# Reordering the lead of an attention and two-MoE kernel, and rounding the first expert's weights on GpSimd

## The chip, the cores and the metric

The kernel runs on one core of a Trainium2 chip. The metric is the device time of one execution in microseconds (us), lower is better. The engines are TensorE (PE in the profile; its weight loads are PEld), VectorE (DVE), ScalarE (ACT) and GpSimd (POOL), each with its own queue of instructions that runs in order; nearly all DMAs are issued by SyncE (SP), also in order.

## The reference

Three blocks follow one another: attention over pooled keys and values, a mixture layer with a rational function, and a gated layer.

```python
# q, k, v: 8 batches, 8 heads, 576 positions, 64 wide
k_p = k.reshape(B, H, Sp, 8, D).mean(axis=3)
v_p = v.reshape(B, H, Sp, 8, D).mean(axis=3)
scores = scale * np.matmul(q, k_p.transpose(0, 1, 3, 2))
scores = scores - np.max(scores, axis=-1, keepdims=True)
attn = np.exp(scores)
attn = attn / (np.sum(attn, axis=-1, keepdims=True) + 1e-09)
x = np.matmul(attn, v_p)                       # -> 4608 tokens x 512
h = x @ w_in                                   # 512 -> 2048
g = (a0 + a1*h + a2*h*h + a3*h**3) / (1 + |b0|*|h| + |b1|*h*h + 1e-6)
x = g @ w_out                                  # 2048 -> 512
out = (sigmoid(x @ w_gate) * (x @ w_val)) @ w_out2   # 512 -> 1536 -> 512
```

The weights arrive as 64-bit numbers.

## The kernel before

**Arithmetic.** Every large product is made of three passes: a number is split into a high part that TensorE's format holds and a low part, and the products low x high, high x high and high x low are added in one PSUM bank (`mm3`, L498 to L502).

**Weights.** Each 512-column piece of a weight is loaded raw (`wi_load`, `wo_load`, 512 KB, L122 and L124 for SyncE). `conv1` turns the 64-bit words into 32-bit floats: two ScalarE operations at once (L92, L94), and, deferred to the next call of `gap()`, a shift on VectorE (L100) and an integer addition on GpSimd (L102). `conv2` makes the two parts: the high part `wh` is a ScalarE copy that rounds (L117), the low part `wl` a subtraction (L118). For the pieces of `w_in` (`wi`) the subtraction runs on VectorE, for those of `w_out` (`wo`) on GpSimd. `weights_a(p)` issues, for step p, `wi_conv2(p+3)`, `wo_conv2(p)`, `wi_conv1(p+5)`, `wo_conv1(p+2)`, `wi_load(p+8)`, `wo_load(p+5)`, in this order, as far as such pieces (0 to 15) exist.

**Steps.** Time is a list of steps written out by hand. The lead, steps -8 to -1, does the attention of the first block of 512 tokens (tiles 0 to 3 of 128 tokens, tile 4 belongs to the next block) and starts the weights. Then 144 steps follow: step n computes a hidden product of 128 x 512 (`g1`, 12 matmuls) and the second product of step n-3 (`g2`, 12 matmuls). The rational function of step n is `rational1` (ScalarE L541, L542; VectorE L543 to L545), `rational2` (ScalarE L551, L552, L554: a reciprocal by logarithm and exponential) and `rational3` (VectorE L558 to L560); `split_g` makes the parts of g (ScalarE L525, GpSimd L528) during the next step. `gap()` is called between `rational2` and `rational3`. `weights_a(n)` stands at the end of the steps 0 to 15.

**Banks.** Four PSUM banks rotate among hidden products (a bank is free when L560 is done), scores (two banks a tile, free when VectorE's L382 is done), transposes of the attention weights (two, free when ScalarE's L410 has copied them) and attention outputs.

**Attention of a tile**, over several steps: scores (L369), maximum and subtraction on VectorE (L380, L382), exponential (ScalarE L388), then `normalise`: sums, sum and reciprocal on VectorE (L395, L397, L398) and the multiply on GpSimd (L399); transposes (L406) copied by ScalarE (L410); the product with v (L421), written as two parts by ScalarE (L426) and VectorE (L427). Each piece of work has a step, a rank and a part: in the lead, part 0 of the elementwise work of a step (`run(off_pe, st, 0)`) comes before part 1. In steps 3, 6, 9 and 12 a tile is normalised, in steps 2, 5, 8 and 11 scores are taken.

**Pooling.** The keys' pooling is a VectorE reduction (L318); `pool_v0(c)` pools chunk c of the first batch's v, chunks 0 and 1 on GpSimd (L348, L349) and chunks 2 and 3 on VectorE (L351); later batches' v is pooled on GpSimd (L335, L336), two chunks of the second batch in step -1 and three in step 0, then, for the third batch, chunks from step 10 on.

**Loads at the start.** SyncE issues 13 loads of the first batch, then `RA` = 3 loads of the second batch's k, then the parameters (L761, L762); in step -7 it issues NCH = 5 further loads into buffers that the first loads leave free.

Of the kernel before, what the change touches and what calls it, by code (L numbers as in the profile page):

```python
# [13 lines left out]
AF = mybir.ActivationFunctionType  # L14
# [21 lines left out]
def attention_moe_glu_kernel(ctx: ExitStack, tc: tile.TileContext, q, k, v, w_in, w_out, ca, cb, w_gate, w_val, w_out2, out):  # L36
    nc = tc.nc
# [8 lines left out]
    NJ = H // 2  # L46
# [63 lines left out]
    def gap():  # L110
        for f in between:
            f()
        between.clear()

    def conv2(raw, wh, wl, eng=nc.gpsimd):
        t = raw[:, :, 1].bitcast(F32)
        nc.scalar.activation(wh, t, AF.Copy)  # L117
        eng.tensor_tensor(out=wl, in0=t, in1=wh.bitcast(F32), op=ALU.subtract)  # L118

    def load_raw(raw, src, by_cols):  # L120
# [48 lines left out]
    def wo_stream(f):  # L169
        wo[f] = slot(wo_tag(f), F32R, "wo")  # L170
        nc.sync.dma_start(wo[f].bitcast(F32).rearrange("p h x -> p (h x)"), wod[f])
# [59 lines left out]
    with tc.manual_schedule():  # L231
# [25 lines left out]
        RA = 3  # L257
# [6 lines left out]
        def early(shape, name):  # L264
            spare[0] = (spare[0] + 1) % len(later)
            pool, tag = later[spare[0]]
            return pool.tile(shape, F32, tag=tag, name=name)

        def load_unit(start=False, tag=None):
            if loaded[0] == len(units):  # L270
                return
            u = units[loaded[0]]
            loaded[0] += 1
            if tag:
                t = tag[0].tile([P, 4 * P], F32, tag=tag[1], name="raw1")
            elif start:
                t = early([P, 8 * P if u[0] == "v" else 4 * P], "raw0")
            else:
                t = raw_p.tile([P, 4 * P], F32, tag="raw", name="raw")
            if u[0] == "q":  # L280
                b, t0, n = tiles[u[1]]
                o = (b * S + t0) * H * D
                nc.sync.dma_start(t[:, :NJ * n], q[o:o + n * H * D].rearrange("(p x) -> p x", p=P))
            elif u[0] == "k":
                cols = k_cols(u[2])
                nc.sync.dma_start(t[:, :(cols.stop - cols.start) * POOL], k[u[1], :, cols.start * POOL:cols.stop * POOL])
            elif u[1] == 0:

                nc.sync.dma_start(t[:SP].rearrange("p (h x) -> p h x", h=2),
                                  v[0][2 * u[2]:2 * u[2] + 2].rearrange("h (s j) d -> s h (j d)", j=POOL))  # L290
            else:
                rows = v[u[1]].rearrange("h (s j) d -> (h s) (j d)", j=POOL)
                c = u[2]
                m = P if c < NCH - 1 else CL
                nc.sync.dma_start(t[:m], rows[c * P:c * P + m])
            raws[u] = t
            if not start and not tag:
                in_ring.add(u)
# [10 lines left out]
        def k_cols(c):  # L309

            return slice(c * D, min((c + 1) * D, NJ * SP))
# [137 lines left out]
        def put(step, rank, pe, rest, gen, *a, use=()):  # L449
            plan.append((step, rank, len(plan), pe, rest, gen(*a), use))  # L450
# [16 lines left out]
        s0 = at[0]  # L467
        for c in range(NCH):
            put(s0 - 4, 0, 0, 0, ew, pool_k, 0, c, use=[("k", 0, c)])
        for c in range(NJ):  # L470
            put(s0 - 2, 5, 0, c >= NJ // 2, ew, pool_v0, c, use=[("v", 0, c)])
        put(s0 - 4, 1, 0, 0, ew, place_k, 0)
        for b in range(1, B):
            e0, e1 = max(at[first[b - 1]], -2), at[last[b - 1]]
            for c in range(2 * NCH):
                w, f = (("k", pool_k), ("v", pool_v))[c // NCH]
                st = e0 + c * (e1 - (3 if w == "k" else 1) - e0) // (2 * NCH)
                if b == 1 and w == "k":
                    st = c // 2 - 4
# [7 lines left out]
        lead = plan[0][0]  # L487
# [5 lines left out]
        def run(which, step, part):  # L493
            for gen in which.get((step, part), []):
                next(gen, None)
# [37 lines left out]
        def g1(n):  # L533
            i, f = divmod(n, NF1)
            ys[n] = hidden(wi[f], xs[i])

        def rational1(n):
            h = ys[n]
            s, u, y = new_tmp("s", "su", 3), new_tmp("u", "su", 3), new_tmp("y", "y", 3)

            nc.scalar.activation(u, h, AF.Abs, scale=coef[:, 5:6])  # L541
            nc.scalar.activation(y, h, AF.Identity, scale=coef[:, 3:4], bias=coef[:, 2:3])  # L542
            nc.vector.scalar_tensor_tensor(out=u, in0=u, scalar=coef[:, 4:5], in1=h, op0=ALU.add, op1=ALU.mult)  # L543
            nc.vector.tensor_tensor(out=y, in0=h, in1=y, op=ALU.mult)
            nc.vector.scalar_tensor_tensor(out=y, in0=y, scalar=coef[:, 1:2], in1=h, op0=ALU.add, op1=ALU.mult)  # L545
            ys[n] = (h, s, u, y)

        def rational2(n):

            h, s, u, y = ys[n]  # L550
            nc.scalar.activation(u, u, AF.Abs)  # L551
            nc.scalar.activation(s, u, AF.Ln, scale=2.0 ** LSH, bias=ONE * 2.0 ** LSH)  # L552

            nc.scalar.activation(h, s, AF.Exp, scale=-1.0, bias=LSH * math.log(2.0))  # L554

        def rational3(n):
            r, s, u, y = ys[n]
            nc.vector.scalar_tensor_tensor(out=y, in0=y, scalar=coef[:, 0:1], in1=r, op0=ALU.add, op1=ALU.mult)  # L558
            nc.vector.scalar_tensor_tensor(out=r, in0=u, scalar=ONE, in1=r, op0=ALU.add, op1=ALU.mult)
            nc.vector.scalar_tensor_tensor(out=y, in0=r, scalar=-2.0, in1=y, op0=ALU.add, op1=ALU.mult)  # L560

        def split_g(n):
            y = ys.pop(n)[3]
            gs[n] = g = g_p.tile([P, 2, TB], F32R, tag="g", name="g")
            split_hi(g, y)
            split_lo(g, y, nc.gpsimd)

        def g2(n):
            i, f = divmod(n, NF1)
            if f == 0:  # L570
                new_acc(i)
            g, wt = gs.pop(n), wo[f]
            for e in range(NJ):
                es = slice(e * P, (e + 1) * P)
                mm3(acc[i][e], wt[:, 1, es], wt[:, 0, es], g[:, 1], g[:, 0], f == 0, f == NF1 - 1)

        def g2_out(n):
            i, f = divmod(n, NF1)
            if f == NF1 - 1:
                for e in range(NJ):  # L580
                    store(acc[i][e], x2d[i][:, e], e < 3, *(("su", 3) if e == NJ - 1 else ()))
# [16 lines left out]
        def ring_load(t):  # L598

            s_, j = divmod(t % (7 * NS), 7)  # L600
            if t < NP * NS * 7:
                ring[t] = wp.tile([P, 2, 4 * P], F32R, tag=f"wi{t % NQ}", name="wq")
                nc.sync.dma_start(ring[t].bitcast(F32), w2d[s_][:, 2 * j:2 * j + 2])
# [152 lines left out]
        nstart = NCH + NJ + n0  # L756
        for i in range(nstart):
            load_unit(True)
        for i in range(RA):
            load_unit()  # L760
        nc.sync.dma_start(pc[:, 0:4], ca.rearrange("(o n) -> o n", o=1).to_broadcast([P, 4]))  # L761
        nc.sync.dma_start(pc[:, 4:6], cb.rearrange("(o n) -> o n", o=1).to_broadcast([P, 2]))  # L762

        def weights_a(p):

            for ahead, f, n in ((3, wi_conv2, NF1), (0, wo_conv2, NF1), (5, wi_conv1, NF1), (2, wo_conv1, NF1),
                                (8, wi_load, NF1), (5, wo_load, NF1)):
                if 0 <= p + ahead < n:
                    f(p + ahead)

        for st in range(lead, 0):
            run(on_pe, st, 0)
            run(on_pe, st, 1)
            run(off_pe, st, 0)
            run(off_pe, st, 1)
            if st == lead + 1:

                for x in range(NCH):
                    load_unit(tag=later[4 + x])
            weights_a(st)  # L780
            gap()

        nc.scalar.activation(coef[:, 0:4], pc[:, 0:4], AF.Copy, scale=-1.0)
        nc.scalar.activation(coef[:, 4:6], pc[:, 4:6], AF.Abs)
# [1 line left out]
        for n in range(N1):  # L786
            m = n - LAG
            if n == N1 - NF1:
                att.close()
                late = ctx.enter_context(tc.tile_pool(name="late", bufs=1))  # L790
            g1(n)
            run(on_pe, n, 0)
            rational1(n)
            run(off_pe, n, 0)
            if n >= 1:
                split_g(n - 1)
            rational2(n)
            run(off_pe, n, 2)
            gap()
            rational3(n)  # L800
            if m >= 0:
                g2(m)
                g2_out(m)
            run(on_pe, n, 1)
            run(off_pe, n, 1)
            if n < NF1:
                weights_a(n)
            elif n % NF1 >= FS:
                wo_stream(n % NF1)
            background(n - NF1)  # L810
            x = n - (N1 - NF1)
            if x == 0:
                rawx = [xs_p.tile([P, 8 * TB], F32, tag="xs", name="rawx")]
                x_load(0)
            if 1 <= x <= NQ:
                ring_load(x - 1)
            if 3 <= x <= 6:
                x_prep(x - 3)
            if x in (4, 5):
                wo2_load(NF1 - NQ + x - 4)  # L820
            if x >= 7:
                wo2_load(x - 7)
# [68 lines left out]
```

## Time and profile before

| | |
|---|---|
| time, median of 3 runs | 1813.69 us (1812.81 to 1815.04) |
| profiled execution: time / span | 1815.3 us / 1813.5 us |
| mean granted TensorE clock | 0.986 |
| TensorE matmul busy | 1761.6 us (97%) |
| VectorE / ScalarE / GpSimd busy | 1104.0 / 975.8 / 801.3 us |
| the chip's DMA mean rate | 173 GB/s |

How to read it: busy times are sums over one profiled execution, and the span runs from its first to its last instruction; the device time is a little longer. The idle time of an engine costs nothing unless it is the one that holds up the others, so the stretches have to be looked at one by one. In the timelines a row has the start in us, the length (of all instructions merged in the row), the engine, the line of the kernel, the operation, what it writes and reads, how many instructions it merges, and in brackets how long the engine had been idle before it and what ended that.

### The profile page before, as it was taken

Reading aid. Unit: us, or ns where it says so; the run is one execution under the profiler, and the core shown is the slowest. Engines: PE = TensorE matmul, PEld = TensorE weight load, DVE = VectorE, ACT = ScalarE, POOL = GpSimd, SP = SyncE. Lnnn points to the kernel's source line nnn. Section 1 sums busy time; section 2 is a strip of 40 time slices with the busy share of each in tenths; the row PEclk is TensorE's granted clock in tenths of the full one; section 3 lists DMA queues with packets and bytes.
Section 4 is the critical chain, followed back from the end, with each engine's and each line's share of the span. In section 5 each row is a group of like instructions: output and inputs, shape, how many; then the busy total and the mean of one; then the engine's idle time right before and its main releaser. Section 6 shows DMA issues by size and latency. Waiting matters only on the chain. (4 is left out here: it accounts for less than half of the span.)

```text
span 1813.5 us, 25319 instructions
## 1 busy us (share of the span) xinstructions
PE 1761.6 (97%) x9056; PEld 1525.1 (84%) x9056; DVE 1104.0 (61%) x1788; ACT 975.8 (54%) x1763; POOL 801.3 (44%) x787
## 2 busy tenths in 40 slices
PE   6699999999999999999999999999999999999999
PEld 5578787788878887788878998998998998998997
DVE  6898887878888888888776333333433333433341
ACT  5998877687877777877875222222222222222221
POOL 3766554563555536634442324324324334334231
PEclk8899999999999999999999999999999999999999
DMA  8564444543544454425465753763763763763660
GB/s 258 169 202 144 151 156 145 195 152 131 202 170 156 139 193 161 168 100 176 167 221 197 236 181 128 236 182 125 240 186 120 240 197 109 238 201 106 206 198 36
DMA packets 128209, 313.60 MB, mean 173 GB/s; under 512 B 16596, under 2 KB 48340, under 8 KB 128084
## 3 DMA queue, kind: packets, MB, share of 16 engines
q1 hardware_dynamic: 128084, 311.99, 52.8%
q8 instruction: 72, 1.18, 0.3%
q14 instruction: 53, 0.43, 0.1%
HBM read 257.95 MB, written 52.95 MB: 171 GB/s over the span
## 5 line engine op out<-in xcount | busy, mean ns | idle before, releaser
L674 DVE TENSOR_TENSOR t<-h,t 128x384 f32<-128x384 f32 x360 | 200.8, 558 | 388.0 <-ACT t L682 273.0
L528 POOL TENSOR_TENSOR g<-y,g 128x512 fp32r<-128x512 f32 x144 | 187.2, 1300 | 283.8 <-ACT g L525 216.6
L727 POOL TENSOR_TENSOR t<-t 128x384 f32<-128x384 f32 x72 | 84.4, 1172 | 449.0 <-issue 253.4
L500 PE MATMUL acc<-g,wo 128*128 128x512 f32 x576 | 233.7, 406 | 0.0
L500 PE MATMUL h<-xs,wi 128*128 128x512 f32 x576 | 231.3, 402 | 2.2 <-DVE xs L427 2.0
L502 PE MATMUL acc<-g,wo 128*128 128x512 f32 x576 | 226.8, 394 | 1.3 <-POOL g L528 1.3
L501 PE MATMUL h<-xs,wi 128*128 128x512 f32 x576 | 226.5, 393 | 0.0
L502 PE MATMUL h<-xs,wi 128*128 128x512 f32 x576 | 226.4, 393 | 0.0
L501 PE MATMUL acc<-g,wo 128*128 128x512 f32 x576 | 226.0, 392 | 0.0
L502 PE MATMUL h<-xS,wq 128*128 128x384 f32 x576 | 193.4, 336 | 0.0
L500 PE MATMUL h<-xS,wq 128*128 128x384 f32 x576 | 193.2, 335 | 0.0
L501 PE MATMUL h<-xS,wq 128*128 128x384 f32 x576 | 193.0, 335 | 0.0
L541 ACT ACTIVATE u<-h,coef 128x512 f32<-128x512 f32 x144 | 98.2, 682 | 104.7 <-PE h L502 104.4
L558 DVE SCALAR_TENSOR_TENSOR y<-y,coef,h 128x512 f32<-128x512 f32 x144 | 107.4, 746 | 75.2 <-ACT h L554 73.0
L543 DVE SCALAR_TENSOR_TENSOR u<-u,coef,h 128x512 f32<-128x512 f32 x144 | 106.4, 739 | 70.9 <-ACT y L542 70.3
L500 PE MATMUL h<-xA,wq 128*128 128x384 f32 x432 | 149.4, 346 | 0.1
L502 PE MATMUL h<-xA,wq 128*128 128x384 f32 x432 | 144.9, 335 | 0.0
L501 PE MATMUL h<-xA,wq 128*128 128x384 f32 x432 | 144.9, 335 | 0.0
L500 PEld LDWEIGHTS h<-xs,wi 128*128 128x128 f32 x576 | 109.7, 191 | 26.8 <-DVE xs L427 3.0
L500 PEld LDWEIGHTS acc<-g,wo 128*128 128x128 f32 x576 | 109.0, 189 | 26.5 <-issue 4.6
L502 PEld LDWEIGHTS acc<-g,wo 128*128 128x128 f32 x576 | 108.9, 189 | 25.6 <-POOL g L528 1.7
L502 PEld LDWEIGHTS h<-xs,wi 128*128 128x128 f32 x576 | 109.3, 190 | 23.8 <-DVE xs L427 0.2
(115 smaller groups left out, 4041.2 us busy)
## 6 DMA issues: line engine op xcount, KB each, us to landing
wq<-w2d SPq DMA_DIRECT2D x252, 512.0 KB
wo<-wod SPq DMA_DIRECT2D x88, 512.0 KB
w2d<-wq SPq DMA_DIRECT2D x36, 512.0 KB
x2d<-o SPq DMA_DIRECT2D x36, 256.0 KB
out_dram<-o SPq DMA_DIRECT2D x36, 256.0 KB
raw<-in_k_dram SPq DMA_DIRECT2D x32, 256.0 KB
raw<-in_q_dram SPq DMA_DIRECT2D x32, 256.0 KB
wiraw<-in_moe_w_in_dram SPq DMA_DIRECT2D x16, 512.0 KB
```

The costliest lines, as they stand in the source:

```text
L500: nc.tensor.matmul(out_, wl, xh, start=start, stop=False, skip_group_check=on)
L501: nc.tensor.matmul(out_, wh, xh, start=False, stop=False, skip_group_check=on)
L502: nc.tensor.matmul(out_, wh, xl, start=False, stop=stop, skip_group_check=on)
L528: eng.tensor_tensor(out=g[:, 1], in0=y, in1=g[:, 0].bitcast(F32), op=ALU.subtract)
L541: nc.scalar.activation(u, h, AF.Abs, scale=coef[:, 5:6])
L543: nc.vector.scalar_tensor_tensor(out=u, in0=u, scalar=coef[:, 4:5], in1=h, op0=ALU.add, op1=ALU.mult)
L558: nc.vector.scalar_tensor_tensor(out=y, in0=y, scalar=coef[:, 0:1], in1=r, op0=ALU.add, op1=ALU.mult)
L674: nc.vector.tensor_tensor(out=out_, in0=a, in1=b, op=ALU.add)
L727: eng.tensor_tensor(out=y, in0=x, in1=y, op=ALU.mult)
```

## The change

- The high part of a `wi` piece is made by GpSimd (`tensor_copy`) where ScalarE made it (L117); VectorE subtracts as before. `wo` pieces are converted as before.
- Chunk 1 of the first batch's v is pooled in part 1 of its step, behind tile 0's normalisation, where it was in part 0, ahead of it. Both are on GpSimd.
- The three `RA` loads leave the place before the parameters and go to the end of step -7; the five NCH loads go from step -7 to the end of step -6. In both steps they now follow `weights_a`.
- `weights_a(-1)`, with `wi_conv2(2)`, `wi_conv1(4)`, `wo_conv1(1)` and the loads of wi 7 and wo 4, leaves the lead and is issued in step 0 after `rational3(0)`. The `gap()` that followed it goes too, so its shifts and additions come with those of `weights_a(0)` in the `gap()` of step 1.

```diff
     def conv2(raw, wh, wl, eng=nc.gpsimd):
         t = raw[:, :, 1].bitcast(F32)
-        nc.scalar.activation(wh, t, AF.Copy)
+        if eng is nc.gpsimd:
+            nc.scalar.activation(wh, t, AF.Copy)
+        else:
+            nc.gpsimd.tensor_copy(wh, t)
         eng.tensor_tensor(out=wl, in0=t, in1=wh.bitcast(F32), op=ALU.subtract)
...
         for c in range(NJ):
-            put(s0 - 2, 5, 0, c >= NJ // 2, ew, pool_v0, c, use=[("v", 0, c)])
+            put(s0 - 2, 5, 0, c >= 1, ew, pool_v0, c, use=[("v", 0, c)])
...
         for i in range(nstart):
             load_unit(True)
-        for i in range(RA):
-            load_unit()
         nc.sync.dma_start(pc[:, 0:4], ca.rearrange("(o n) -> o n", o=1).to_broadcast([P, 4]))
...
             run(off_pe, st, 0)
             run(off_pe, st, 1)
+            if st < -1:
+                weights_a(st)
+                gap()
             if st == lead + 1:
+                for i in range(RA):
+                    load_unit()
+            if st == lead + 2:
                 for x in range(NCH):
                     load_unit(tag=later[4 + x])
-            weights_a(st)
-            gap()
...
             gap()
             rational3(n)
+            if n == 0:
+                weights_a(-1)
             if m >= 0:
                 g2(m)
                 g2_out(m)
```

## Rows read from the trace of the kernel before

**Rows 1.** Busy time by stretch: stretch, length, busy us and count by engine, clock, DMA

```profile
38.50:63.06 24.56, 12.55 (x53) 9.39 (x53) 18.85 (x29) 20.80 (x39) 18.91 (x25) 0.71 0.52 171
63.06:180.00 116.94, 109.81 (x559) 88.56 (x559) 106.05 (x181) 107.35 (x188) 78.31 (x74) 0.95 0.53 175
180.00:300.00 120.00, 116.63 (x583) 94.65 (x582) 97.49 (x160) 92.13 (x165) 62.17 (x69) 0.99 0.47 160
```

**Rows 2.** Waits of TensorE, 63 to 160 us: us in total, times, longest

```profile
PE sc L369 <- ACT aT L410: 4.5, 3, 2.0
```

**Rows 3.** Timeline of ScalarE, steps 3, 4 and 15

```profile
72.60 0.66 ACT L117 ACTIVATE wi<-wiraw 128x512 fp32r<-128x512 f32 x1
...
75.99 0.67 ACT L541 ACTIVATE u<-h,coef 128x512 f32<-128x512 f32 x1
...
156.84 0.69 ACT L541 ACTIVATE u<-h,coef 128x512 f32<-128x512 f32 x1 [1.40 <-PE h L502]
```

**Rows 4.** Timeline of VectorE, steps 2, 3, 4 and 13

```profile
61.94 0.73 DVE L543 SCALAR_TENSOR_TENSOR u<-u,coef,h 128x512 f32<-128x512 f32 x1
...
63.97 0.42 DVE L100 TENSOR_SCALAR wiraw<-wiraw 128x512 int32<-128x512 int32 x1
...
69.52 0.75 DVE L543 SCALAR_TENSOR_TENSOR u<-u,coef,h 128x512 f32<-128x512 f32 x1 [0.61 <-ACT y L542]
...
74.74 0.73 DVE L395 TENSOR_REDUCE r<-e 64x8 f32<-64x576 f32 x1
...
77.35 0.75 DVE L543 SCALAR_TENSOR_TENSOR u<-u,coef,h 128x512 f32<-128x512 f32 x1 [0.89 <-ACT y L542]
...
145.75 0.74 DVE L543 SCALAR_TENSOR_TENSOR u<-u,coef,h 128x512 f32<-128x512 f32 x1
```

**Rows 5.** Timelines of VectorE, GpSimd and TensorE, tiles 0 and 1

```profile
15.04 0.20 DVE L398 RECIPROCAL r<-r 128x8 f32<-128x8 f32 x1
...
17.91 1.15 POOL L399 TENSOR_TENSOR e<-e,r 128x576 f32<-128x576 f32 x1
21.53 1.15 POOL L399 TENSOR_TENSOR e<-e,r 128x576 f32<-128x576 f32 x1 [2.47 <-DVE r L398]
...
23.97 1.07 PE L406 MATMUL pta<-ident,e 128*72 128x128 f32 x8
```

**Rows 6.** Timelines of TensorE, ScalarE and VectorE, first product, steps 0 and 1

```profile
38.50 0.80 PE L500 MATMUL h<-xs,wi 128*128 128x512 f32 x1
...
44.35 0.69 ACT L541 ACTIVATE u<-h,coef 128x512 f32<-128x512 f32 x1
...
54.11 0.75 DVE L543 SCALAR_TENSOR_TENSOR u<-u,coef,h 128x512 f32<-128x512 f32 x1 [2.83 <-ACT y L542]
```

**Rows 7.** Timeline of GpSimd, steps -1 to 3

```profile
42.68 1.76 POOL L399 TENSOR_TENSOR e<-e,r 64x576 f32<-64x576 f32 x1 [3.25 <-DVE r L398]
...
46.21 1.27 POOL L335 TENSOR_TENSOR raw<-raw 128x256 f32<-128x256 f32 x2
47.56 0.32 POOL L336 TENSOR_TENSOR vp<-raw 128x64 f32<-128x64 f32 x1
...
55.17 1.29 POOL L118 TENSOR_TENSOR wo<-woraw,wo 128x512 fp32r<-128x512 f32 x1
...
65.58 1.03 POOL L102 TENSOR_TENSOR woraw<-woraw 128x512 int32<-128x512 int32 x1
...
76.05 1.42 POOL L399 TENSOR_TENSOR e<-e,r 64x576 f32<-64x576 f32 x1 [1.31 <-DVE r L398]
```

**Rows 8.** Timeline of GpSimd, the start

```profile
1.01 0.29 POOL masks.py:199 TENSOR_SCALAR_AFFINE_SELECT ident<-ident 128x128 f32<-128x128 f32 x1
```

**Rows 9.** Timelines of VectorE and GpSimd, subtractions that meet and one alone

```profile
60.22 1.79 DVE L118 TENSOR_TENSOR wi<-wiraw,wi 128x512 fp32r<-128x512 f32 x1
68.24 0.67 DVE L118 TENSOR_TENSOR wi<-wiraw,wi 128x512 fp32r<-128x512 f32 x1
...
60.17 1.30 POOL L118 TENSOR_TENSOR wo<-woraw,wo 128x512 fp32r<-128x512 f32 x1
```

## The prediction, made before the changed kernel ran

> **What bounds the kernel now.** I read the busy time by stretch first. From 180 us on TensorE is busy 117 of 120 us [rows 1], so nothing that happens there can move; all that the change touches lies before 180 us. Between 38.5 and 63 us TensorE works only 12.6 of 24.6 us; between 63 and 180 us it works 109.8 of 116.9 us, and there ScalarE (107) and VectorE (106) are nearly as full as TensorE [rows 1]. A microsecond by which TensorE reaches its dense part sooner or later is a microsecond at the end.
>
> Next the waits of TensorE: most of its 7.1 us of idle time after 63 us ends with ScalarE's L410 [rows 2], so the elementwise chain sets the pace there, not TensorE. Which engine of that chain? ScalarE runs its six conversions after step 3 without a pause, from 72.60 to L541 at 75.99 (0.57 each), and first waits for a hidden product at 156.84 [rows 3]. VectorE, in the same step, is through with its work 0.89 before L543 at 77.35 [rows 4]. ScalarE is the bound, with VectorE under a microsecond behind. The 11 steps from L543 of step 2 (61.94) to L543 of step 13 (145.75) take 83.81, 7.62 each [rows 4].
>
> **The change, front.** GpSimd now normalises tile 0 before it pools v's second chunk. The reciprocal was ready at 15.24 (start plus length), the multiply started only at 17.91 [rows 5]; it can start when the first chunk is through, about 15.4, so TensorE's first transposes come 2.5 earlier. Half of it is lost at tile 1: its multiply waits for VectorE's reciprocal until 21.53, which stands behind two poolings that don't move, and takes 1.15, so its transposes can start at 22.75 where they stood at 23.97, 1.2 earlier [rows 5]. The other two tiles follow that chain, so I carry 1.1 to the first product, 38.50 [rows 6]. On SyncE's queue two weight loads and the parameters now go ahead of three k chunks; k's poolings come after tile 2's sums, so the later landing hides there and I cost it at nothing. If that cover is gone, the 1.1 goes with it.
>
> **The last lead conversion.** Five ScalarE operations stand between the exponential of tile 4 and step 0; without them L541 starts when the product ends. Twelve matmuls from 38.50 end about 42.3, less 1.1 is 41.2, where L541 stood at 44.35 [rows 6]: 3.1 earlier. I give none of that to the end, because step 1 is set by another engine. GpSimd worked without pause from 42.68 to the wo subtraction at 55.17 [rows 7]. It now starts 1.1 earlier, runs its first multiply in 1.15 and not 1.76, and has two integer additions (1.03 each [rows 7]) fewer, but two copies more. Its wo subtraction of step 0 so starts at 55.17 − 1.1 − 0.6 − 2.0 + 1.6 = 53.1, and only then is the rounded part of wi[3] there for VectorE.
>
> **What a copy costs.** No row shows a GpSimd copy of 128x512. The one operation with a single input takes 0.29 for 128 columns [rows 8]. If all of it goes by column, a copy takes 1.16; with a fixed part of 0.22 (two-input operations of 64 and 512 columns take 0.32 and 1.03 [rows 7], 0.71 for 448 columns) it takes 0.50. I take the middle, 0.8. Here the Trainium skill, GPSIMD Engine Reference, Engine selection, speaks for the change: it calls GpSimd slow for two inputs but roughly at line rate for one; its section on side-by-side cycle accounting has 0.77 us for 512 elements in a tight loop, an estimate by which the sum below would be 0.4 less. No run here shows that yet.
>
> **The new wait.** VectorE's wi subtraction (L118) now waits for the copy, and VectorE's whole next step is queued behind it. The copy stands in GpSimd's queue behind both integer additions, and in a normalise step behind that multiply too; behind the copy stands the wo subtraction. The two engines also collide: a VectorE L118 that started 0.05 after a GpSimd L118 took 1.79 and ended 0.54 after it, where one without a rival took 0.67 [rows 9]. GpSimd starts its next operation at once and VectorE must first see the copy's end, so I let GpSimd go first: from the copy's end VectorE needs 1.30 + 0.55.
>
> Entry: L118 of wi[3] ends at 53.1 + 1.30 + 0.55 = 54.95, and L543 of step 1 starts there, 0.8 later than 54.11 [rows 6]. Step 1 then holds the shifts and additions of two steps (four pairs, two of them deferred from the lead). The first shift stands 2.03 after L543 (61.94 to 63.97 [rows 4]), at 56.98; two additions are through 2.64 after that (63.97 to 66.61 [rows 4, 7]), at 59.6. By the collision the third shift gets in only then. Two shifts and the last three operations take 2.8 (L543 to the sums is 5.22 in step 3 [rows 4], less 2.03 and 0.35 for that tile's output), so L560 ends at 62.4. The second pair of additions ends about 62.2, the copy 63.0, the wo subtraction 64.3, VectorE's L118 64.85: L543 of step 2 is 2.9 later than 61.94, and TensorE's third product some 2 later.
>
> Steps 2 to 12: in a plain or scores step the next L543 follows after 2.03 + 2.64 + 0.8 + 1.30 + 0.55 = 7.3. In a normalise step it is 5.22 to the sums (69.52 to 74.74), 1.31 to the multiply (76.05), 1.15 for it, then 0.8 + 1.30 + 0.55: 10.3 [rows 4, 5, 7]. In the two steps with a v pooling besides (1.27 and 0.32 [rows 7]) it is 8.9. Five, four and two of them: 36.6 + 41.3 + 17.8 = 95.7, against 83.81: 11.9 more. ScalarE's gain, one operation of 0.57 in each step, brings nothing, as it is no longer last. When the conversions end, TensorE is the bound; ScalarE's pause of 1.40 at 156.84 [rows 3] says that about 1.5 is made up there.
>
> Sum: 2.9 + 11.9 − 1.5 = 13.3 later. The profiled execution has a span of 1813.5 and a time of 1815.3, so 1828.6; it stands 1.6 above the median of the three runs (1813.69), which gives 1827.0. With the copy at 0.50 or 1.16, 0.30 less to 0.36 more at each of some 13 places, it is 1823 to 1832.
>
> **Rivals.** (a) VectorE gets through first after each copy. Then 0.65 takes the place of 1.85: normalise steps 9.1, steps with a v pooling 7.7, and the other five are set by ScalarE again (7.62 less 0.57, 7.05): 35.3 + 36.5 + 15.4 = 87.2, 3.4 more; entry 0.6 later, made up 1.5: 2.5 later, 1816. The collision [rows 9] speaks against it; that GpSimd's multiply at 42.68 stretched to 1.76 [rows 7] shows that VectorE does get in when it is there first. (b) Faster: the wait is covered. If the copy is done before VectorE's L560 ends, ScalarE stays the bound and is 12 × 0.57 = 6.8 shorter; TensorE can take that, as it has 7.1 idle [rows 1], and the front adds 1.1 while the entry costs about 2: 1808. It decides from the point where GpSimd reaches the copy 0.8 ahead of L560's end; in step 2 the additions ended at 66.61, 2.64 after the first shift, and L560 about 2.8 after it, so the copy lacks 0.6 and, in normalise steps, far more. (c) The change doesn't do what it says at the front: the poolings on VectorE set the pace of all four tiles and the 1.1 isn't there; everything else as forecast, 1828.
>
> **Chances.** The forecast with (c) 0.60, (a) 0.25, (b) 0.10, and 0.05 for a front that gains 2 or 3 more with little wait behind it. About 0.2%, 3.6 us, is what a measurement of this kernel can tell from no change: 1810 to 1817.3. Half of (a) and the last 0.05 fall there: same 0.17. (b) and a little is faster, 0.12; slower 0.71. The range for 8 in 10 leaves out (b) and the uppermost tail: 1812 to 1833. The forecast alone: 1823 to 1832.
>
> **What would show it.** Right: rows of a GpSimd copy of 0.5 to 1.2; L118 on VectorE released by GpSimd, with VectorE idle ahead of it in every step from 0 to 12, for 2 us and more in normalise steps; ScalarE with pauses ahead of L551; L541 of step 0 near 41 and L543 of step 2 near 65; waits of TensorE of 15 to 20 us between 63 and 160. Wrong: L118 of 0.65 right behind the copy (a); ScalarE without a pause up to step 13 at some 7.1 a step (b); the first product not near 37.4 (c).

## The result and the profile after

The changed kernel takes 1825.07 us (median of 4 runs, 1823.04 to 1828.06), the kernel before, timed beside it, 1813.25 us (4 runs, 1811.73 to 1815.04): a ratio of 1.007, 95% interval 1.0056 to 1.0084, so 11.8 us slower. The profiled spans, 1826.3 and 1813.5 us, differ by 12.8.

The busy time by stretch of the changed kernel, cut where the same work begins and ends (first product, third step's product, 180 us in the trace of before), with the columns of [rows 1]:

```profile
37.12:63.87 26.75, 14.93 (x54) 11.06 (x53) 19.51 (x29) 19.22 (x36) 20.72 (x29) 0.69 0.62 209
63.87:192.40 128.53, 112.82 (x560) 89.88 (x560) 111.02 (x181) 101.41 (x177) 84.03 (x85) 0.93 0.46 151
192.40:312.40 120.00, 116.89 (x591) 94.85 (x589) 99.02 (x164) 92.25 (x165) 62.21 (x69) 1.00 0.48 162
```

The second row holds the loss: 128.5 us for work that took 116.9 [rows 1], with TensorE's idle time at 15.7 where it was 7.1; the other 3.0 are longer matmuls, at a mean granted clock of 0.93 for 0.95. ScalarE is busy 101 us where it was 107: it lost the copies and nothing came of it. The third row is as full as before.

What VectorE waited for in the changed kernel from 63 to 160 us (us in total, times, longest) is one thing alone:

```profile
DVE wi L121 <- POOL wi L120: 10.4, 7, 2.0
```

In the kernel before it waited half as long in that stretch, and for ScalarE alone:

```profile
DVE u L543 <- ACT y L542: 5.1, 7, 1.1
DVE y L558 <- ACT h L554: 0.2, 1, 0.2
```

(The line numbers of the changed kernel are 3 or 4 higher: L120 is the GpSimd copy, L121 the subtraction, L547 what was L543, L545 what was L541, L555 what was L551, L398 and L402 the normalisation's sums and multiply, L532 the low part of g. The kernels of the experiments have numbers of their own.)

Steps 3 and 4 in VectorE's timeline of the changed kernel (start, length, instruction, idle time and releaser):

```profile
69.78 0.75 DVE L547 SCALAR_TENSOR_TENSOR u<-u,coef,h 128x512 f32<-128x512 f32 x1
...
75.00 0.73 DVE L398 TENSOR_REDUCE r<-e 64x8 f32<-64x576 f32 x1
...
78.06 3.04 DVE L121 TENSOR_TENSOR wi<-wiraw,wi 128x512 fp32r<-128x512 f32 x1 [1.90 <-POOL wi L120]
81.02 0.73 DVE L547 SCALAR_TENSOR_TENSOR u<-u,coef,h 128x512 f32<-128x512 f32 x1
...
86.33 1.77 DVE L121 TENSOR_TENSOR wi<-wiraw,wi 128x512 fp32r<-128x512 f32 x1 [0.38 <-POOL wi L120]
88.03 0.73 DVE L547 SCALAR_TENSOR_TENSOR u<-u,coef,h 128x512 f32<-128x512 f32 x1
```

The same time in GpSimd's timeline:

```profile
73.95 1.04 POOL L102 TENSOR_TENSOR woraw<-woraw 128x512 int32<-128x512 int32 x1
76.30 1.15 POOL L402 TENSOR_TENSOR e<-e,r 64x576 f32<-64x576 f32 x1 [1.31 <-DVE r L401]
77.39 0.63 POOL L120 CAST wi<-wiraw 128x512 fp32r<-128x512 f32 x1
77.99 1.31 POOL L121 TENSOR_TENSOR wo<-woraw,wo 128x512 fp32r<-128x512 f32 x1
79.26 1.29 POOL L532 TENSOR_TENSOR g<-y,g 128x512 fp32r<-128x512 f32 x1
```

Read together they are step 3, with the wait and the collision that were forecast. VectorE has its sums at 75.00 and the reciprocal 1.2 later, then stands idle for 1.90 while GpSimd multiplies and copies. The copy ends at 78.02; GpSimd starts the wo subtraction at once, VectorE starts at 78.06, and its subtraction, alone 0.67 long [rows 9], ends only at 81.10, 0.55 after GpSimd's second operation. In the kernel before, the same subtraction followed the reciprocal at once and went ahead of GpSimd's multiply at 76.05 [rows 7]:

```profile
75.83 0.63 DVE L118 TENSOR_TENSOR wi<-wiraw,wi 128x512 fp32r<-128x512 f32 x1
```

Step 3 takes 11.24 (69.78 to 81.02), where it took 7.83 [rows 4]. ScalarE's row at the other end of the chain says the same; the first row is of the kernel before:

```profile
78.13 0.64 ACT L551 ACTIVATE u<-u 128x512 f32<-128x512 f32 x1 [0.29 <-DVE u L543]
```

```profile
81.79 0.63 ACT L555 ACTIVATE u<-u 128x512 f32<-128x512 f32 x1 [4.23 <-DVE u L547]
```

ScalarE pauses for 4.23 us where it had paused for 0.29.

### The profile page after: what moved, and what is told of

It reads as the page before. It is cut to its first block, busy times and chain, and to the rows that moved or that the text cites. A ratio compares the mean times of both kernels' runs of the same rounds, so it can differ in the third digit from the quotient of the medians.

```text
span 1826.3 us, 25314 instructions
## 1 busy us (share of the span) xinstructions
PE 1765.5 (97%) x9056; PEld 1526.3 (84%) x9056; DVE 1109.3 (61%) x1788; ACT 967.6 (53%) x1747; POOL 810.4 (44%) x803
## 4 chain that ended last, share of the span: by engine, by line
PE 74%; DVE 6%; ACT 6%; POOL 6%; issue 4%; DMA 2%; SPq 0%; POOLq 0%; ACTq 0%; DVEq 0%
PE h L504 14%; PE h L506 14%; PE h L505 14%; PE acc L504 5%; PE acc L506 4%; PE acc L505 4%; PE accA L742 3%; PE accA L743 3%; PE h L742 3%; PE h L743 3%; PE accA L741 3%; PE h L741 3%; DMA w2d<-wq 2%; PE psx L424 1%; POOL g L532 1%
## 5 line engine op out<-in xcount | busy, mean ns | idle before, releaser
L532 POOL TENSOR_TENSOR g<-y,g 128x512 fp32r<-128x512 f32 x144 | 189.1, 1313 | 280.6 <-ACT g L529 219.7
L545 ACT ACTIVATE u<-h,coef 128x512 f32<-128x512 f32 x144 | 98.3, 683 | 104.5 <-PE h L506 104.4
L547 DVE SCALAR_TENSOR_TENSOR u<-u,coef,h 128x512 f32<-128x512 f32 x144 | 106.2, 737 | 64.2 <-ACT y L546 63.6
L504 PEld LDWEIGHTS acc<-g,wo 128*128 128x128 f32 x576 | 108.6, 188 | 26.2 <-issue 4.6
```

The source lines that it names most:

```text
L504: nc.tensor.matmul(out_, wl, xh, start=start, stop=False, skip_group_check=on)
L532: eng.tensor_tensor(out=g[:, 1], in0=y, in1=g[:, 0].bitcast(F32), op=ALU.subtract)
```

## The experiments

All are read by the starts of VectorE's first rational operation (L543 of before) in each step, in one trace of each kernel. The table has the time from one step's start to the next's, the sum from step 2 to 13, and, last, the time from the start of the first product to step 2, which in the kernel before is 23.44 (61.94 less 38.50).

| kernel | 2 | 3 | 4 | 5 | 6 | 7 | 8 | 9 | 10 | 11 | 12 | sum | product to step 2 |
|---|---|---|---|---|---|---|---|---|---|---|---|---|---|
| before | 7.58 | 7.83 | 7.51 | 8.17 | 7.50 | 7.54 | 7.97 | 8.04 | 7.56 | 7.42 | 6.69 | 83.81 | 23.44 |
| changed | 7.08 | 11.24 | 7.01 | 8.08 | 10.47 | 7.00 | 7.66 | 10.03 | 8.61 | 8.64 | 9.69 | 95.51 | 25.58 |
| reordering alone | 8.23 | 7.83 | 7.54 | 8.17 | 7.53 | 7.55 | 7.99 | 8.03 | 7.53 | 7.41 | 6.68 | 84.49 | 25.44 |
| GpSimd copies alone | 7.13 | 11.19 | 7.00 | 8.10 | 10.36 | 7.01 | 7.65 | 10.04 | 8.61 | 8.64 | 9.70 | 95.43 | 27.51 |
| copy issued early | 7.23 | 7.12 | 8.54 | 8.08 | 7.48 | 8.31 | 7.23 | 8.99 | 6.98 | 7.87 | 6.96 | 84.79 | 25.91 |
| ScalarE in long steps | 7.11 | 7.83 | 7.50 | 8.08 | 7.54 | 8.12 | 7.23 | 7.76 | 7.57 | 7.43 | 7.87 | 84.04 | 25.64 |
| wo first | 7.19 | 11.03 | 7.16 | 8.09 | 11.59 | 7.16 | 7.93 | 11.40 | 8.78 | 9.89 | 10.93 | 101.15 | 25.96 |
| two copies | 7.74 | 10.49 | 7.71 | 8.09 | 11.08 | 7.71 | 7.78 | 10.73 | 9.31 | 9.33 | 10.40 | 100.37 | 29.69 |

**The reordering alone.**

```diff
# against the changed kernel
     def conv2(raw, wh, wl, eng=nc.gpsimd):
         t = raw[:, :, 1].bitcast(F32)
-        if eng is nc.gpsimd:
-            nc.scalar.activation(wh, t, AF.Copy)
-        else:
-            nc.gpsimd.tensor_copy(wh, t)
+        nc.scalar.activation(wh, t, AF.Copy)
```

> The changed kernel with the high parts of wi rounded by ScalarE again: the reordering alone. Theory (VectorE's wait for the GpSimd copy costs the time, step by step): the 83.8 us from L543 of step 2 to that of step 13 are those of before, the first product starts about 1.4 earlier, as in the changed kernel (37.12 against 38.50), and the doubled shifts and additions of step 1 give back 2 to 3, so 0 to 2 slower than before, about 1814. Rival (the reordering, by what it defers into step 1, is the loss): most of the 12 us stays, 1822 to 1826.

Measured: 1813.02 us against 1812.93 of before, ratio 1.000 (0.999 to 1.001); 84.49 from step 2 to 13. The loss is not in the reordering, which as a whole changes nothing that can be measured.

**The GpSimd copies alone.**

```diff
# against the kernel before
     def conv2(raw, wh, wl, eng=nc.gpsimd):
         t = raw[:, :, 1].bitcast(F32)
-        nc.scalar.activation(wh, t, AF.Copy)
+        if eng is nc.gpsimd:
+            nc.scalar.activation(wh, t, AF.Copy)
+        else:
+            nc.gpsimd.tensor_copy(wh, t)
```

> The kernel before with nothing changed but GpSimd rounding the high parts of wi. Theory: the steps 2 to 13 take 95 to 96 us as in the changed kernel (95.51) instead of 83.81, 11.7 more, and the lead without the reordering adds 0 to 2: 1825 to 1828. Rival (reordering is the loss): ScalarE is relieved by 13 x 0.57, so 0 to 6 us faster, 1807 to 1813.

Measured: 1828.19 us against 1812.93, ratio 1.0081 (1.006 to 1.0102); 95.43 from step 2 to 13, every step within 0.11 of the changed kernel's. VectorE's timeline of its step 3:

```profile
78.89 3.03 DVE L121 TENSOR_TENSOR wi<-wiraw,wi 128x512 fp32r<-128x512 f32 x1 [1.91 <-POOL wi L120]
```

The wait and the doubly lost subtraction are there without any reordering. The two runs together place all of the loss in one edit.

Up to step 2 this kernel loses more than the changed one, 27.51 for 25.58. Here a copy still stands in the last step of the lead, in GpSimd's queue behind poolings of v, and VectorE waits for it:

```profile
44.89 0.69 DVE L121 TENSOR_TENSOR wi<-wiraw,wi 128x512 fp32r<-128x512 f32 x1 [5.14 <-POOL wi L120]
```

In the changed kernel that conversion is deferred; the other two edits of the reordering leave this stretch as it was, at 23.4 in their own runs below. With the copies the deferral is thus a gain of 1.9, while by itself it is a loss of 1.9: the two edits do not add up.

**The copy issued early.** Same copies, same engine, ahead of the step's integer additions and not behind them and the normalisation.

```diff
# against the changed kernel; wi_conv2 split into wi_high (the copy) and the subtraction
+            if 2 <= n and n + 3 < NF1:
+                wi_high(n + 3)
             rational2(n)
             run(off_pe, n, 2)
             gap()
```

> The changed kernel with the GpSimd copy of step n issued ahead of that step's integer additions, behind the low part of g, from step 2 on; the same copies on the same engines. Theory (what costs is the place of the copy in GpSimd's queue, with VectorE waiting and then losing to the wo subtraction): VectorE no longer waits for a copy in steps 2 to 12, ScalarE is the bound again and one operation (0.57) a step shorter, so 78 to 82 us from step 2 to 13; with 0.8 lost up to step 2 some 1808 to 1812, faster than before. Rival (GpSimd's 0.64 us more in each step, or its use of the shared port, is what costs wherever it stands): 1818 to 1826.

Measured: 1815.35 us against 1812.93, ratio 1.0013 (1.0002 to 1.0023); 84.79 from step 2 to 13. The 11.7 us of the steps shrink to 1.0 with all copies still on GpSimd, so their place in the queue costs, and not their work. But the expected gain over before, with 78 to 82 in these steps, did not come. VectorE no longer waits for a copy in these steps, yet ScalarE's shorter steps bring nothing, because VectorE, with only 2.9 us of waits left between 63 and 160 us, now loses the time elsewhere. Its timeline in step 4, and GpSimd's:

```profile
78.34 1.87 DVE L100 TENSOR_SCALAR wiraw<-wiraw 128x512 int32<-128x512 int32 x1
80.12 1.87 DVE L100 TENSOR_SCALAR woraw<-woraw 128x512 int32<-128x512 int32 x1
```

```profile
77.35 1.32 POOL L121 TENSOR_TENSOR wo<-woraw,wo 128x512 fp32r<-128x512 f32 x1
78.64 1.28 POOL L538 TENSOR_TENSOR g<-y,g 128x512 fp32r<-128x512 f32 x1
79.87 0.84 POOL L154 CAST wi<-wiraw 128x512 fp32r<-128x512 f32 x1
80.67 1.04 POOL L102 TENSOR_TENSOR wiraw<-wiraw 128x512 int32<-128x512 int32 x1
```

Two shifts of 0.42 [rows 4] take 1.87 each, beside four GpSimd operations that follow one another without a gap: the first shift ends 0.29 after the low part of g, having met the wo subtraction (here L121) before it, the second 0.28 after the addition, having met the copy (L154) before it. Step 4 takes 8.54.

**ScalarE in the long steps.**

```diff
# against the changed kernel
-    def conv2(raw, wh, wl, eng=nc.gpsimd):
+    def conv2(raw, wh, wl, eng=nc.gpsimd, hi=None):
...
-        if eng is nc.gpsimd:
+        if eng is nc.gpsimd or hi:
             nc.scalar.activation(wh, t, AF.Copy)
...
-        conv2(wi_raw.pop(f), wi[f][:, 0], wi[f][:, 1], nc.vector)
+        conv2(wi_raw.pop(f), wi[f][:, 0], wi[f][:, 1], nc.vector, f - 3 in (3, 6, 9, 10, 11, 12))
```

> The changed kernel, but ScalarE rounds the high part in steps 3, 6, 9, 10, 11 and 12, in which the copy stands behind a normalisation or a pooling of v on GpSimd; the plain and scores steps keep the GpSimd copy. Theory: those six steps cost what they did before (10.0 to 11.2 and 8.6 in the changed kernel against 7.5 to 8.0), the other five keep their 7.0 to 8.1, which is no more than before; all of the 11.7 us goes and 1 to 2 besides: 1811 to 1815. Rival (every copy costs the same): 6 of 11 copies gone, about half of the loss stays, 1818 to 1820.

Measured: 1814.99 us against 1812.93, ratio 1.0004 (0.9994 to 1.0013); 84.04 from step 2 to 13. Six copies off GpSimd remove the whole loss, and five copies left there cost nothing: a copy costs where a normalisation or a pooling of v stands ahead of it on GpSimd. The 1 to 2 us that were expected besides did not come: the five steps with a copy are 0.7 shorter together than before, but step 12 is 1.2 longer, because ScalarE there waits for TensorE's product:

```profile
143.85 0.69 ACT L545 ACTIVATE u<-h,coef 128x512 f32<-128x512 f32 x1 [1.32 <-PE h L506]
```

**The wo conversion first.**

```diff
# against the changed kernel
-            for ahead, f, n in ((3, wi_conv2, NF1), (0, wo_conv2, NF1), (5, wi_conv1, NF1), ...
+            for ahead, f, n in ((0, wo_conv2, NF1), (3, wi_conv2, NF1), (5, wi_conv1, NF1), ...
```

> The changed kernel with the wo conversion of a step issued ahead of the wi conversion, so that on GpSimd the wo subtraction (1.30) comes before the copy (0.64) and nothing of the weights stands behind the copy. Theory (the wait and the collision behind it are both paid): VectorE waits 1.30 longer but then subtracts in 0.67, without the collision that takes 1.78 (3.04 in step 3); 1.30 + 0.64 + 0.67 = 2.61 for 0.64 + 1.78 = 2.42 a step, and 1.25 less in the step that collides twice: steps 2 to 13 take 95 to 98, time within 3 of the changed kernel, 1823 to 1828. Rival (the collision costs nothing, the wait for the queue is all): 1.30 more in each of 11 steps, 108 to 110 from step 2 to 13, 1836 to 1840.

Measured: 1832.57 us against 1811.82, ratio 1.0112 (1.0095 to 1.0129); 101.15 from step 2 to 13, between the two expectations, and both ranges are missed. VectorE's timeline, steps 3 and 4:

```profile
78.38 1.76 DVE L121 TENSOR_TENSOR wi<-wiraw,wi 128x512 fp32r<-128x512 f32 x1 [3.17 <-POOL wi L120]
...
86.61 0.69 DVE L121 TENSOR_TENSOR wi<-wiraw,wi 128x512 fp32r<-128x512 f32 x1 [1.62 <-POOL wi L120]
```

In the plain step 4 it went as the theory has it: 1.24 more of waiting (1.62 for 0.38), but a subtraction of 0.69 in place of 1.77, and 7.16 for 7.01 in all. So the collision is a real part of the price. In the normalise step the wait grew by 1.27 and the subtraction still met GpSimd, this time the low part of g, which was ready because ScalarE had run ahead; there the theory was wrong. Step 3 met one operation fewer than in the changed kernel and is no longer than there; steps 6, 9, 11 and 12, 1.1 to 1.4 longer each, make 5.0 of the 5.6 us by which the sum is over the changed kernel's.

**Two copies.**

```diff
# against the changed kernel
             nc.gpsimd.tensor_copy(wh, t)
+            nc.gpsimd.tensor_copy(wh, t)
```

> The changed kernel with every GpSimd copy issued twice, one behind the other, to the same place. Theory (VectorE behind GpSimd's queue sets the pace of every step): each of the steps 2 to 12 grows by the 0.6 of a copy, 6.6 to 7 in all, and one or two in the lead and steps 0 and 1: steps 2 to 13 take 101 to 103, time 1831 to 1834. Rival (ScalarE or TensorE sets the pace and the loss comes from the lead): GpSimd, busy 44%, takes it in, 1824 to 1827.

Measured: 1834.06 us against 1811.82, ratio 1.0122 (1.0103 to 1.0142); 100.37 from step 2 to 13, 4.9 more than the changed kernel and a little under the 101 to 103 expected. Eight of the eleven steps grow by 0.6 to 0.7, the whole of a copy; the scores steps 5 and 8 hardly grow, and step 3 shrinks by 0.75, because its subtraction meets one GpSimd operation and not two (it takes 1.78 for 3.04); step 2 stands 4.1 later against the first product. In the steps in which VectorE waits for it, a GpSimd copy goes through nearly one for one.

**Parts of the reordering**, each against the kernel before, one execution each. The three edits, in this order: the deferred conversions, the normalisation, the loads.

```diff
+            if st < -1:
+                weights_a(st)
+                gap()
...
             rational3(n)
+            if n == 0:
+                weights_a(-1)
```

```diff
-            put(s0 - 2, 5, 0, c >= NJ // 2, ew, pool_v0, c, use=[("v", 0, c)])
+            put(s0 - 2, 5, 0, c >= 1, ew, pool_v0, c, use=[("v", 0, c)])
```

```diff
-        for i in range(RA):
-            load_unit()
...
+            weights_a(st)
+            gap()
             if st == lead + 1:
+                for i in range(RA):
+                    load_unit()
+            if st == lead + 2:
                 for x in range(NCH):
                     load_unit(tag=later[4 + x])
-            weights_a(st)
-            gap()
```

> The kernel before with only the last lead step's conversions deferred into step 0, behind the rational function. Theory: L541 of step 0 starts when the first product ends, 2 to 3 earlier than before, and L543 of step 2 is 0.5 to 2 later than before against the start of the first product, as step 1 holds four shifts and four additions; from step 2 on the steps take 83 to 85. Rival (deferring is a gain that lasts): step 2 starts 1 to 3 earlier.

> The kernel before with only the pooling of v's second chunk behind tile 0's normalisation. Theory: tile 0's transposes start about 6.5 after the first scores instead of 9.3 (19.11 less 9.82), the first product 1.0 to 1.5 earlier against the first scores (before: 28.7 later), and step 2 follows it with the same gain. Rival (vh on VectorE and slower weights take it back): the first product not earlier than 28.4 after the first scores.

> The kernel before with only the second batch's loads moved behind the first weights' conversions and loads. Theory (loads are no term of the sum): the first product 28.0 to 29.4 after the first scores (before: 28.7), L543 of step 2 51.5 to 53.0 after them (52.1), steps 2 to 13 as before (83.8). Rival (the loads are what helps at the front): first product under 28.0.

Their times, 1816.24, 1810.67 and 1813.27 us, are of one execution each. The kernel before took 1809.08 to 1814.05 beside the first two and 1810.25 to 1816.17 beside the third, so only the deferral's stands out.

The first scores start anywhere from 7.6 to 9.8 us in these executions, with no edit to what comes ahead of them, so the front is measured from there: to tile 0's transposes, to the first product, to step 2.

| kernel | to the transposes | to the first product | to step 2 |
|---|---|---|---|
| before | 9.29 | 28.68 | 52.12 |
| deferred conversions alone | 9.70 | 29.70 | 55.02 |
| normalisation alone | 6.78 | 27.85 | 51.28 |
| loads alone | 9.26 | 28.33 | 51.75 |
| changed | 7.04 | 27.91 | 53.49 |

Deferring lets step 0 follow the first product by 5.03 instead of 7.24 on VectorE, but takes 25.32 from the first product to step 2 (55.02 less 29.70) for 23.44, a loss of 1.9. The rows of its step 1 on VectorE:

```profile
55.83 0.42 DVE L100 TENSOR_SCALAR wiraw<-wiraw 128x512 int32<-128x512 int32 x1
56.16 0.42 DVE L100 TENSOR_SCALAR woraw<-woraw 128x512 int32<-128x512 int32 x1
56.50 1.26 DVE L100 TENSOR_SCALAR wiraw<-wiraw 128x512 int32<-128x512 int32 x1
57.68 1.26 DVE L100 TENSOR_SCALAR woraw<-woraw 128x512 int32<-128x512 int32 x1
58.86 0.73 DVE L558 SCALAR_TENSOR_TENSOR y<-y,coef,h 128x512 f32<-128x512 f32 x1
```

Four shifts take 3.03 (55.83 to 58.86); the second pair meets the additions of the first. The normalisation gives 2.5 at the transposes, as forecast, and 0.8 at the first product, less than the 1.0 to 1.5 expected. The 2.5 is clear: in all traces with the normalisation first the transposes come 6.8 to 7.3 after the first scores, in all without it 8.7 to 9.7. The 0.8, and the 0.35 of the loads, are not clear by themselves: the two kernels of the next experiment are alike up to step 2, and their first products stand 27.99 and 26.71 after the first scores. Over all traces the mean is 27.2 for the nine with the normalisation first (26.2 to 28.0) and 28.6 for the four without (27.7 to 29.7).

**Without the deferral, and with copies in plain steps alone.** The normalisation and the loads together, and the same with this edit:

```diff
# against the kernel before
-    def conv2(raw, wh, wl, eng=nc.gpsimd):
+    def conv2(raw, wh, wl, eng=nc.gpsimd, hi=nc.scalar):
...
-        nc.scalar.activation(wh, t, AF.Copy)
+        if hi is nc.scalar:
+            nc.scalar.activation(wh, t, AF.Copy)
+        else:
+            nc.gpsimd.tensor_copy(wh, t)
...
-        conv2(wi_raw.pop(f), wi[f][:, 0], wi[f][:, 1], nc.vector)
+        conv2(wi_raw.pop(f), wi[f][:, 0], wi[f][:, 1], nc.vector,
+              nc.gpsimd if f - 3 in (2, 4, 5, 7, 8) else nc.scalar)
```

> The kernel before with tile 0's normalisation ahead of the second pooling and with the loads moved; no deferred conversion, no GpSimd copy. Theory: the front's gain of 0.8 (as in the run with the normalisation alone) goes through to the end, as steps 2 to 13 stay 83.8: 0.5 to 1.5 faster than before, 0.9991 to 0.9997, which 5 rounds may just not tell from none. Rival (later loads or the pooling of v take it back): 1.000 and above.

> As the kernel with normalisation and loads moved, but GpSimd rounds the high part of wi in steps 2, 4, 5, 7 and 8, where neither a normalisation nor a pooling of v stands ahead of the copy. Theory: those five steps become 0 to 0.5 shorter (7.0 to 8.1 against 7.5 to 8.2), some 1 us in all, and 0.8 from the front: 1 to 2.5 faster than before, 0.9986 to 0.9995. Rival (each GpSimd copy costs, wherever it stands): 3 to 5 us slower, 1.0015 to 1.003.

Measured: 1810.42 us against 1812.91 for the first, ratio 0.9989 (0.9981 to 0.9998), and 1809.47 for the second, 0.9985 (0.9976 to 0.9993). Both are a little faster than the kernel before. The steps from 2 to 13 are 83.93 and 83.62, so what is gained is gained ahead of step 2. The times gain 2.5 and 3.4 us, more than the rows show there (step 2 stands 51.46 and 50.17 after the first scores, for 52.12), and the first more than the 0.5 to 1.5 expected; where the rest comes from is open. The five steps with GpSimd copies take 38.82 together, where they take 38.83 without: the 1 us expected of them did not come, and they cost nothing, which refutes the rival.

## Why the prediction was right, point by point

The forecast was 1827 us, 13.3 later than before; it is 1825.07, 11.8 later by the medians and 12.8 by the spans. The mechanism is shown: the copies alone give the loss, the reordering alone doesn't, and moving the copies in GpSimd's queue or out of the long steps takes it away. The size owes something to luck, as the terms show one by one:

**The steps 2 to 12: 11.9 forecast, 11.7 measured** (95.51 less 83.81), and step for step: the plain steps 4 and 7 take 7.0 (forecast 7.3), the scores steps 2, 5 and 8 take 7.1, 8.1 and 7.7 (7.3), the normalise steps 9.7 to 11.2 (10.3), those with a v pooling 8.6 (8.9). The plain and v steps are shorter in part by what the copy is: 0.64 and not the 0.8 taken between 0.50 and 1.16. In the scores steps the forecast had the wrong path: the copy is done before VectorE is through with its own work, and VectorE waits for nothing. That the five plain and scores steps come to 36.8 for the 36.6 forecast is luck. The Trainium skill's figure (GPSIMD Engine Reference, the section on side-by-side cycle accounting, 0.77 us for 512 elements) lies above it.

**The collision.** GpSimd did go first behind the copy: in 7 of the 11 steps the subtraction took 1.64 to 1.80, in step 3 even 3.04; that it can lose twice in a row was not in the forecast. In the scores steps 2, 5 and 8 it came later and stood nearly alone (0.68 to 0.79), which the forecast had not told apart from the plain ones. Collisions as such were not new: the kernel before had them too, in step 4 for one, where the subtraction took 1.82 and still ended ahead of ScalarE. New is that ScalarE is no longer later than they are, so that they set the step.

**The front: 1.1 forecast; 0.8 against the first scores.** By the two timelines it is 1.4 (37.12 for 38.50), but 0.6 of that is first scores that started at 9.21 for 9.82. Traces of like kernels differ by more than 0.3 here, so the forecast is neither confirmed nor denied in its size. L541 of step 0 came at 41.41 for the forecast 41.2.

**The entry was mis-sized: 2.9 forecast, 0.8 measured** (L543 of step 2 at 62.70 for 64.85). Two things. GpSimd reached the wo subtraction of step 0 at 51.59, not 53.1: its multiply of tile 4 began at 40.87 and so 1.8 and not 1.1 before 42.68 [rows 7], and the two copies took 0.3 less than reckoned. And in step 1 the third shift did not wait for both additions. VectorE's timeline and GpSimd's in the changed kernel:

```profile
56.06 1.26 DVE L100 TENSOR_SCALAR wiraw<-wiraw 128x512 int32<-128x512 int32 x1
57.25 1.26 DVE L100 TENSOR_SCALAR woraw<-woraw 128x512 int32<-128x512 int32 x1
```

```profile
55.89 1.15 POOL L102 TENSOR_TENSOR wiraw<-wiraw 128x512 int32<-128x512 int32 x1 [1.19 <-DVE wiraw L100]
57.00 1.22 POOL L102 TENSOR_TENSOR woraw<-woraw 128x512 int32<-128x512 int32 x1
58.18 1.22 POOL L102 TENSOR_TENSOR wiraw<-wiraw 128x512 int32<-128x512 int32 x1
```

The shift at 56.06 ended at 57.32, 0.28 after the first addition (57.04), and it is the second addition that was stretched, to 1.22 for 1.03. Here VectorE got in between two GpSimd operations that stood back to back. Against the first product, where the start of the scores does not enter, the entry was forecast as 4.0 (2.9 and the 1.1 of the front) and measured as 2.1 (25.58 less 23.44).

**What is made up: 1.5 forecast, nothing measured.** From step 13 to 18 the distance to the kernel before stays at 12.4 to 12.5. I read it so: ScalarE's pause at 156.84 [rows 3] was not slack that could be given back; it showed TensorE as the bound there, and TensorE had just been held up by the same 12 us.

So the total rests on two errors that cancelled, an entry 2.1 too dear and 1.5 of recovery that doesn't exist; the central term and its cause stood.

**The signs named beforehand.** The copy of 0.64 lies in its range, VectorE's subtraction is released by GpSimd, and ScalarE pauses ahead of L555 (17.6 us from 63 to 160, 1.3 before). Three signs failed in part. VectorE stood idle ahead of its subtraction in 7 of the steps 2 to 12 and not in all. In the normalise steps it did so for 1.84 to 1.90 and not 2 and more. TensorE's waits from 63 to 160 add up to 12.2 and not 15 to 20, where they were 7.0 before.

**The rivals.** (a), VectorE first behind the copy, is refuted by the rows of 1.77 and 3.04. (b), ScalarE's 0.57 a step as a gain, did not come even in the run that took the wait away: VectorE was the next bound, and there the price of (b) was too good by all of its 6.8 us. The trace of before already said so: of the 11 starts of L543 in steps 3 to 13 only six waited for ScalarE, 4.2 us in all, and at the other five VectorE itself was the last. The prediction had read it off one step, where the wait was 0.89, and called ScalarE the bound of all. (c), a front without gain, is spoken against by the transposes, the means of the first product and the time of the run with the normalisation and the loads (0.9981 to 0.9998); no single pair of traces refutes it.

## What to carry to other kernels

An operation given to an engine with free time is paid by whoever waits for it: read what stands ahead of it in that engine's queue and what of the waiting engine is queued behind the wait, not the engine's busy share. GpSimd was 44% busy, its copy took 0.64 us, and the copies cost 12 us. Relieving the bound of a chain is worth no more than the distance to the next engine of it, here under a microsecond a step, and it needs a place in which the new wait is covered.

## What was not expected of the hardware

An operation of VectorE that meets GpSimd at SBUF may lose more than once: in step 3 its subtraction took 3.04, past two GpSimd operations. The Trainium skill (SBUF — State Buffer, the section on the two separate sides) has it that of a VectorE operation with two inputs in SBUF and a GpSimd operation that reads SBUF, whichever starts first holds the shared pair of ports for its whole instruction; the rows agree as far as the first operation goes, with the subtraction ending 0.5 to 0.6 after GpSimd's. Who comes next where GpSimd's operations stand back to back is not settled. Step 3 was the exception: in steps 6, 9, 11 and 12 of the changed kernel the same two GpSimd operations follow one another, and there VectorE came in between and the low part of g was stretched from 1.29 to 1.73 and more, as in step 6:

```profile
104.87 1.78 DVE L121 TENSOR_TENSOR wi<-wiraw,wi 128x512 fp32r<-128x512 f32 x1 [1.84 <-POOL wi L120]
```

```profile
104.80 1.31 POOL L121 TENSOR_TENSOR wo<-woraw,wo 128x512 fp32r<-128x512 f32 x1
106.07 1.73 POOL L532 TENSOR_TENSOR g<-y,g 128x512 fp32r<-128x512 f32 x1
```

The shifts show both outcomes too: VectorE got in at 57.0 in the changed kernel, while in the kernel before a shift of step 1 went past the wo subtraction at 55.17 [rows 7] and the low part of g behind it:

```profile
56.16 1.82 DVE L100 TENSOR_SCALAR wiraw<-wiraw 128x512 int32<-128x512 int32 x1
```

```profile
56.42 1.27 POOL L528 TENSOR_TENSOR g<-y,g 128x512 fp32r<-128x512 f32 x1
```

The first scores start at 7.6 to 9.8 us in the thirteen traces, one of each kernel, and kernels that are alike up to there differ, so a gain of a microsecond at the front can't be read from the starts of two profiles alone.
